# A SwiGLU layer on one core: the last row tile in two column groups, and two of four turned stores behind the next cast

## The chip, the core and the metric

The kernel runs on one core of a Trainium2 chip. The metric is the device time of one execution in microseconds (us). "Before" is the kernel as it stood, "after" the kernel with the change.

## What is computed

```python
B, S, D, F = 1, 2048, 640, 1536      # all bf16, random
def reference(x, w_gate, w_up, w_down):
    g = _silu(x @ w_gate)            # 2048 x 1536
    u = x @ w_up                     # 2048 x 1536
    return (g * u) @ w_down          # 2048 x 640
```

## The kernel before

The 2048 rows are worked through in four blocks of 512 rows (the loop over `sb`, line 271), called stages here. The contraction dimension lies on the 128 partitions: `xT` holds x turned, in 5 slices of 128 of the 640 input columns, and `aT` holds the hidden activations turned, in 12 slices of 128 of the 1536 hidden columns.

**Projections.** For each of the 12 hidden slices, TensorE (PE) makes 5 matmuls for the gate into a PSUM tile `pg` and 5 for the up projection into `pu` (lines 204 and 277 to 278). ScalarE (ACT) applies silu to `pg` (line 221), VectorE (DVE) multiplies by `pu` and writes a slice of `aT` (line 222). The first block has an order of its own in `head()`. The last 4 rows of x are not projected on TensorE: VectorE works them out as dot products with copies of the weights that DMAs have turned (`row_dots`, line 153), spread over the stages with `do_dots(n)`; `row_tail` (lines 167 and 168) writes their activations.

**Output.** The 640 output columns are made in two ways.

- *Columns 512 to 639, turned* (lines 284 to 305). 12 matmuls, with `wd_sb` as the weights, make a tile `po_t` of 128 columns by the block's 512 rows (384 in the last stage). ACT casts it to bf16 (`ot_t`, line 296), DVE turns its 32 x 32 blocks (`ot_q`, line 298), and four DMAs, one for each 32 columns, store it (line 300). These four *turned stores* are issued from ACT's own queue, one after the other: ACT does nothing behind them until they are issued, and the first waits for DVE's turn.
- *Columns 0 to 511* (lines 307 to 334). For each of the block's four row tiles of 128 rows (`j`), 12 matmuls with `aT` as the weights make a PSUM tile `po_a` of 128 x 512 (line 316). ACT casts it (`ot`, line 325), and SyncE (SP) issues its store (line 334). The tag `po_a` has two PSUM buffers, so the third row tile's matmuls need the first row tile's cast to be done, and the fourth need the second's.

The very last row tile is another matter, for there the turned tile holds 384 rows only. Its 640 columns are made in three groups, of 256, 256 and 128 columns (line 312), 12 matmuls each. ACT casts the first two (line 325), DVE the narrow third (`ot_b`, line 328), and SP issues the three stores.

**What sets the order.** Within one engine, instructions run in the order in which they stand. `keep_order` fixes the traced order for DVE and SP at the end of the program (lines 339 and 340), and for PE, ACT and POOL at the end of `head()` alone (lines 266 to 268); behind that, a scheduler places them. SP's queue holds, besides the stores, all large loads; in the first stage a load of x and the turned loads of `w_up` stand behind the fourth row tile's store (lines 335 to 338). DMAs from SP and ACT take eight completion semaphores in turn, and a DMA waits for the previous user of the semaphore that it gets. `_trim` leaves one closing wait on SP (line 414 in the profile), for everything that was started.

Of the kernel before, what the change touches and what calls it, by code (L numbers as in the profile page):

```python
# [10 lines left out]
def _body(  # L11
# [9 lines left out]
    P = nc.NUM_PARTITIONS  # L21
# [5 lines left out]
    B, S0, D = x.shape  # L27
# [10 lines left out]
    DA = 512  # L38
    Q = 32
# [70 lines left out]
    def turn_x(c0, c1, k0=0, k1=KD):  # L110
        s_sl = slice(c0 * P, c1 * P)
        nc.sync.dma_start_transpose(out=xT[:, k0:k1, s_sl], in_=xt_v[s_sl, k0:k1])
# [22 lines left out]
    def turn_w(dst, src):  # L135
        for a in range(0, KF, WT_STEP):
            nc.sync.dma_start_transpose(
                out=dst[:, a : a + WT_STEP, :], in_=src[:, a : a + WT_STEP, :]
            )
# [24 lines left out]
    def row_tail():  # L164
        for _ in dots:
            pass
        nc.scalar.activation(row_s[:], row_g[:], ACT.Silu)
        nc.vector.tensor_tensor(
            out=aT[:, :, S - T : S], in0=row_s[:], in1=row_u[:], op=ALU.mult
        )  # L170
# [3 lines left out]
    def do_dots(n):  # L174
        for _ in range(n):
            next(dots, None)
# [25 lines left out]
    def proj(ps, w_sb, fc, sb, c0, c1, k0=0, k1=KD):  # L202
        for kd in range(k0, k1):
            nc.tensor.matmul(  # L204
                ps[:, c0:c1],
                lhsT=w_sb[:, kd, fc * P : (fc + 1) * P],
                rhs=xT[:, kd, sb * S_BLK + c0 : sb * S_BLK + c1],
                start=(kd == 0),
                stop=(kd == KD - 1),
            )  # L210

    def gu_tiles():
        pg = psum.tile([P, S_BLK], f32, tag="gu", name="pg", bufs=4)
        pu = psum.tile([P, S_BLK], f32, tag="gu", name="pu", bufs=4)
        return pg, pu

    def gate(pg, pu, sb, fc, n_s):

        s0 = sb * S_BLK
        sg = work.tile([P, S_BLK], f32, name="sg")  # L220
        nc.scalar.activation(sg[:, 0:n_s], pg[:, 0:n_s], ACT.Silu)  # L221
        nc.vector.tensor_tensor(  # L222
            out=aT[:, fc, s0 : s0 + n_s], in0=sg[:, 0:n_s], in1=pu[:, 0:n_s], op=ALU.mult
        )
# [46 lines left out]
    for sb in range(NSB):  # L271
        n_s = S_BLK if sb < NSB - 1 else S_BLK - T
        for fc in range(KF):
            if sb == 0 and fc < N_FIRST:
                continue
            pg, pu = gu_tiles()
            proj(pg, wg_sb, fc, sb, 0, n_s)
            proj(pu, wu_sb, fc, sb, 0, n_s)
            gate(pg, pu, sb, fc, n_s)
            if sb > 0 and fc < KF - 2:  # L280
                do_dots(2)


        n_t = (SUB if sb < NSB - 1 else SUB - 1) * P
        po_t = psum.tile([P, n_t], f32, tag="po_b", name="po_t")
        for kf in range(KF):
            nc.tensor.matmul(  # L287
                po_t[:],
                lhsT=wd_sb[:, kf, DA:D],
                rhs=aT[:, kf, sb * S_BLK : sb * S_BLK + n_t],  # L290
                start=(kf == 0),
                stop=(kf == KF - 1),
            )
        ot_t = outp.tile([P, n_t], bf16, name="ot_t")
        ot_q = outp.tile([P, n_t], bf16, name="ot_q")
        nc.scalar.copy(ot_t[:], po_t[:])  # L296
        do_dots(3)
        nc.vector.transpose(out=ot_q[:], in_=ot_t[:])  # L298
        for q in range(P // Q):
            nc.scalar.dma_start(  # L300
                out=out2[
                    sb * S_BLK : sb * S_BLK + n_t, DA + q * Q : DA + (q + 1) * Q
                ].rearrange("(i r) c -> r i c", r=Q),
                in_=ot_q[q * Q : (q + 1) * Q, :].rearrange("r (i c) -> r i c", c=Q),
            )

        for j in range(SUB):
            s0 = sb * S_BLK + j * P
            last = sb == NSB - 1 and j == SUB - 1
            cols = [(0, DA, "po_a")]  # L310
            if last:
                cols = [(0, DA // 2, "po_a"), (DA // 2, DA, "po_a"), (DA, D, "po_b")]
            for c0, c1, tag in cols:
                po = psum.tile([P, c1 - c0], f32, tag=tag, name="po_a")
                for kf in range(KF):
                    nc.tensor.matmul(  # L316
                        po[:],
                        lhsT=aT[:, kf, s0 : s0 + P],
                        rhs=wd_sb[:, kf, c0:c1],
                        start=(kf == 0),  # L320
                        stop=(kf == KF - 1),
                    )
                ot = outp.tile([P, c1 - c0], bf16, name="ot" if c1 < D else "ot_b")
                if c1 < D:
                    nc.scalar.copy(ot[:], po[:])  # L325
                    eng = nc.sync
                else:
                    nc.vector.tensor_copy(out=ot[:], in_=po[:])  # L328
                    eng = nc.sync
                if 0 < j and not last:  # L330
                    do_dots(3)
                if sb == NSB - 1 and j == ROW_J:
                    row_tail()
                eng.dma_start(out=out2[s0 : s0 + P, c0:c1], in_=ot[:])
        if sb == 0:
            turn_x(2 * SUB, 3 * SUB)
            turn_w(wuT, wut_v)
            turn_x(3 * SUB, 4 * SUB)
# [72 lines left out]
def kernel(tc, *args):  # L411
    _body(tc, *args)
    tc.close()
    tc.compile()
    _trim(tc.nc)
# [30 lines left out]
```

## Time and profile before

| what | us |
|---|---|
| time, median of 3 runs (163.05 to 163.59) | 163.4 |
| the profiled execution's own time | 163.25 |
| its span, first to last instruction | 161.9 |
| PE busy | 159.6 |
| DVE busy | 110.5 |
| ACT busy | 42.6 |
| PE, output row tiles (line 316), 216 matmuls | 42.8 |

A row of a timeline has the start, the duration, the engine, the line, the operation and its operands, a count, and in brackets how long the engine was idle ahead of it and what ended that. "SPq" and "ACTq" are the issue of a DMA by that engine, which takes the engine's queue for the duration given; the transfer itself comes later, and "to landing" is the time from the issue to the arrival of its completion. A row of the chain has a start, a duration, an engine, a tile and a line. A row of grouped instructions has its busy time in us, the mean of one in ns, and the idle time ahead. A row of stretches gives a stretch and its length, then the busy time and count of PE, DVE and ACT, the granted clock of TensorE, the busy share of the DMA engines, and GB/s. Matmuls overlap: the next one starts before the one ahead has ended, so a duration of 0.38 goes with a start every 0.216.

### The profile page before, as it was taken

How to read it: one execution, taken by the hardware profiler on the slowest of the kernel's cores; microseconds unless marked ns; L12 is line 12 of the kernel's file. 1: busy time of each engine (PE TensorE's matmuls, PEld its weight loads, DVE VectorE, ACT ScalarE, POOL GpSimd, SP SyncE). 2: the span in 40 equal slices, each digit the busy share in tenths (PEclk: the TensorE clock that was granted, in tenths of full speed). 3: DMA queues.
4: the chain of work that ended last, by engine and by line, in shares of the span. 5: the costliest groups of instructions: out<-in, count | busy, mean ns of one | idle time of the engine just before them, and what ended most of it. 6: DMA issues, size and time to landing. Idle time of an engine off the chain costs nothing.

```text
span 161.9 us, 2159 instructions
## 1 busy us (share of the span) xinstructions
PE 159.6 (99%) x818; PEld 79.9 (49%) x818; DVE 110.5 (68%) x249; ACT 42.6 (26%) x74; POOL 0.6 (0%) x6
## 2 busy tenths in 40 slices
PE   9999999999999999999999999999999999999995
PEld 9885444444444444444444444444444444445454
DVE  1006223599469999989919999979964999993000
ACT  5032222112222222211222322221214222222121
POOL 1000000000000000000000000000000000000000
PEclk9999999999999999999999999999999999999999
DMA  7999999995089992003110000000310000000212
GB/s 228 280 345 348 363 209 241 230 190 100 32 186 139 241 225 58 0 0 34 65 65 4 0 0 2 0 0 4 64 66 32 0 0 0 0 4 0 52 37 73
DMA packets 41209, 15.86 MB, mean 98 GB/s; under 512 B 33264, under 2 KB 41072, under 8 KB 41200
## 3 DMA queue, kind: packets, MB, share of 16 engines
q1 hardware_dynamic: 32832, 14.81, 38.0%
q10 hardware_dynamic: 8368, 0.92, 3.7%
q8 instruction: 6, 0.10, 0.3%
q14 instruction: 3, 0.02, 0.1%
HBM read 6.88 MB, written 2.62 MB: 59 GB/s over the span
## 4 chain that ended last, share of the span: by engine, by line
PE 99%; DVE 0%; issue 0%
PE pu L204 32%; PE pg L204 31%; PE po_a L316 26%; PE po_t L287 6%; PE pg L250 2%; PE pw L182 1%; PE pt L195 1%; DVE ot_b L328 0%; DVE ones L108 0%
## 5 line engine op out<-in xcount | busy, mean ns | idle before, releaser
L204 PE MATMUL pu<-xT,wu_sb 128*128 128x512 bf16 (+2 forms) x260 | 59.3, 362 | 0.0
L204 PE MATMUL pg<-xT,wg_sb 128*128 128x512 bf16 (+2 forms) x240 | 56.9, 370 | 0.0
L222 DVE TENSOR_TENSOR aT<-sg,pu 128x512 bf16<-128x512 f32 (+1 forms) x48 | 32.5, 682 | 32.8 <-PE pu L204 32.8
L221 ACT ACTIVATE sg<-pg 128x512 f32<-128x512 f32 (+1 forms) x48 | 28.4, 597 | 71.1 <-PE pg L204 67.5
L316 PE MATMUL po_a<-wd_sb,aT 128*128 128x512 bf16 (+2 forms) x216 | 42.8, 358 | 0.0
L153 DVE SCALAR_TENSOR_TENSOR prod<-wgT,x_row 128x640 f32<-128x640 bf16 x48 | 39.4, 821 | 1.1
L153 DVE SCALAR_TENSOR_TENSOR prod<-wuT,x_row 128x640 f32<-128x640 bf16 x48 | 39.4, 822 | 1.0
L204 PEld LDWEIGHTS <-wu_sb 128*128 128x128 bf16 x260 | 25.4, 98 | 26.5 <-DMA wu_sb<-in_w_up_dram 0.2
L204 PEld LDWEIGHTS <-wg_sb 128*128 128x128 bf16 x240 | 23.5, 98 | 25.9
L316 PEld LDWEIGHTS <-aT 128*128 128x128 bf16 x216 | 20.7, 98 | 21.6
L325 ACT CAST ot<-po_a 128x512 bf16<-128x512 f32 (+1 forms) x17 | 9.5, 561 | 32.0 <-PE po_a L316 20.9
L287 PE MATMUL po_t<-aT,wd_sb 128*128 128x512 bf16 (+1 forms) x48 | 10.4, 366 | 0.0
L287 PEld LDWEIGHTS <-wd_sb 128*128 128x128 bf16 x48 | 4.7, 98 | 5.1
L328 DVE CAST ot_b<-po_a 128x128 bf16<-128x128 f32 x1 | 0.3, 292 | 9.9 <-PE po_a L316 9.9
L296 ACT CAST ot_t<-po_t 128x512 bf16<-128x512 f32 (+1 forms) x4 | 2.2, 559 | 11.6 <-PE po_t L287 11.6
L153 DVE DVE_READ_ACCUMULATOR prod<-wuT,x_row 128x1 f32 x48 | 4.0, 82 | 0.0
L153 DVE DVE_READ_ACCUMULATOR prod<-wgT,x_row 128x1 f32 x48 | 3.9, 82 | 0.0
L298 DVE STREAM_TRANSPOSE ot_q<-ot_t 128x512 bf16<-128x512 bf16 (+1 forms) x4 | 2.7, 678 | 1.7 <-ACT ot_t L296 1.7
L250 PE MATMUL pg<-xT,wg_sb 128*128 128x256 bf16 (+1 forms) x24 | 3.1, 307 | 0.0
L200 DVE COPY xT<-pt 128x384 bf16<-128x384 bf16 x2 | 0.7, 358 | 3.2 <-PE pt L195 3.2
L250 PEld LDWEIGHTS <-wg_sb 128*128 128x128 bf16 x24 | 2.6, 127 | 0.3
L182 PE MATMUL pw<-ones 128*128 128x128 bf16 x20 | 2.3, 313 | 0.3 <-DVE ones L108 0.3
(15 smaller groups left out, 8.0 us busy)
## 6 DMA issues: line engine op xcount, KB each, us to landing
wd_sb<-in_w_down_dram SPq DMA_DIRECT2D x1, 1920.0 KB, 14.6
out_dram<-ot SPq DMA_DIRECT2D x15, 128.0 KB, 1.7
wg_sb<-in_w_gate_dram SPq DMA_DIRECT2D x2, 640.0 KB, 6.7
wu_sb<-in_w_up_dram SPq DMA_DIRECT2D x2, 640.0 KB, 8.0
x_row<-in_x_dram SPq DMA_DIRECT2D x1, 640.0 KB, 4.9
wg_sb<-in_w_gate_dram SPq DMA_DIRECT2D x3, 128.0 KB, 3.5
wu_sb<-in_w_up_dram SPq DMA_DIRECT2D x1, 384.0 KB, 4.7
out_dram<-ot_q ACTq DMA_DIRECT2D x12, 32.0 KB, 2.1
```

The costliest lines, as they stand in the source:

```text
L153: nc.vector.scalar_tensor_tensor(out=prod[:], in0=wT[:, fc, :], scalar=1.0, in1=x_row[:, t, :], op0=ALU.mult, op1=ALU.mult, accum_out=acc[ ...
L182: nc.tensor.matmul(pw[:, 0:P], lhsT=ones[:].broadcast_to([P, P]), rhs=ones[:].broadcast_to([P, P]), start=True, stop=True,)
L195: nc.tensor.transpose(out=pt[:, kd - k0, :], in_=x_sb[:, c, kd * P : (kd + 1) * P], identity=ident[:],)
L204: nc.tensor.matmul(ps[:, c0:c1], lhsT=w_sb[:, kd, fc * P : (fc + 1) * P], rhs=xT[:, kd, sb * S_BLK + c0 : sb * S_BLK + c1], start=(kd == 0 ...
L221: nc.scalar.activation(sg[:, 0:n_s], pg[:, 0:n_s], ACT.Silu)
L222: nc.vector.tensor_tensor(out=aT[:, fc, s0 : s0 + n_s], in0=sg[:, 0:n_s], in1=pu[:, 0:n_s], op=ALU.mult)
L250: nc.tensor.matmul(pg[:, c0:c1], lhsT=wg_sb[:, kd, wslice(fc, fc + 1)], rhs=xT[:, kd, c0:c1], start=(kd == 0 and c0 == 0), stop=(kd == KD ...
L287: nc.tensor.matmul(po_t[:], lhsT=wd_sb[:, kf, DA:D], rhs=aT[:, kf, sb * S_BLK : sb * S_BLK + n_t], start=(kf == 0), stop=(kf == KF - 1),)
L296: nc.scalar.copy(ot_t[:], po_t[:])
L298: nc.vector.transpose(out=ot_q[:], in_=ot_t[:])
L316: nc.tensor.matmul(po[:], lhsT=aT[:, kf, s0 : s0 + P], rhs=wd_sb[:, kf, c0:c1], start=(kf == 0), stop=(kf == KF - 1),)
L325: nc.scalar.copy(ot[:], po[:])
```

## The change

The last row tile is made in two column groups, of 512 and 128, in place of 256, 256 and 128. And of the four turned stores of a stage two are traced as before, behind the turn, and two behind the cast of the stage's first row tile.

```diff
         nc.vector.transpose(out=ot_q[:], in_=ot_t[:])
-        for q in range(P // Q):
+
+        def store_q(q):
             nc.scalar.dma_start(
...
             )
 
+        late_q = list(range(P // Q // 2, P // Q))
+        for q in range(P // Q // 2):
+            store_q(q)
+
         for j in range(SUB):
             s0 = sb * S_BLK + j * P
             last = sb == NSB - 1 and j == SUB - 1
             cols = [(0, DA, "po_a")]
             if last:
-                cols = [(0, DA // 2, "po_a"), (DA // 2, DA, "po_a"), (DA, D, "po_b")]
+                cols = [(0, DA, "po_a"), (DA, D, "po_b")]
...
                 if c1 < D:
                     nc.scalar.copy(ot[:], po[:])
+                    while late_q:
+                        store_q(late_q.pop(0))
                     eng = nc.sync
```

As built, three stages have on ACT: two turned stores, the first row tile's cast, two turned stores, three casts. The last stage has three turned stores, the first cast, one turned store, three casts.

## The prediction, written before the changed kernel ran

> **What bounds the kernel now.** I read the page first (span, busy times, chain of work that ended last), then the chain in order of time, then the timeline of the last 12 us, since both halves of the change lie there or beside TensorE's work.
>
> ```profile
> span 161.9 us, 2159 instructions
> ...
> PE 159.6 (99%) x818; PEld 79.9 (49%) x818; DVE 110.5 (68%) x249; ACT 42.6 (26%) x74; POOL 0.6 (0%) x6
> ...
> PE 99%; DVE 0%; issue 0%
> ```
>
> ```profile
> 33.15 10.36 PE po_a L316 x48
> ...
> 148.86 11.07 PE po_a L316 x72
> 159.93 0.02 issue
> 159.95 0.29 DVE ot_b L328
> ```
>
> The reader is to see one engine: TensorE is busy 99% of the span, and the chain runs over its matmuls without a gap until 159.93 us. A step counts in two ways only: it makes TensorE work or wait longer, or it moves what stands behind TensorE's last matmul, some 2 us of cast, store and landing. That tail is this:
>
> ```profile
> 156.66 0.59 ACT L325 CAST ot<-po_a 128x512 bf16<-128x512 f32 x1 [2.00 <-PE po_a L316]
> 158.02 0.37 ACT L325 CAST ot<-po_a 128x256 bf16<-128x256 f32 x1 [0.77 <-PE po_a L316]
> 159.33 0.37 ACT L325 CAST ot<-po_a 128x256 bf16<-128x256 f32 x1 [0.94 <-PE po_a L316]
> ```
>
> ```profile
> 159.72 0.33 SPq L334 DMA_DIRECT2D out_dram<-ot  x1
> 159.95 0.29 DVE L328 CAST ot_b<-po_a 128x128 bf16<-128x128 f32 x1 [9.88 <-PE po_a L316]
> 160.27 0.33 SPq L334 DMA_DIRECT2D out_dram<-ot_b  x1
> ```
>
> ```profile
> out_dram<-ot SPq DMA_DIRECT2D x15, 128.0 KB, 1.7
> out_dram<-ot SPq DMA_DIRECT2D x2, 64.0 KB, 1.5
> out_dram<-ot_b SPq DMA_DIRECT2D x1, 32.0 KB, 1.5
> ```
>
> ```profile
> SPq L414 <- DMA out_dram<-ot: 0.5, 1, 0.5
> ...
> SPq L414 <- DMA out_dram<-ot_b: 0.4, 1, 0.4
> ```
>
> The last 64 KB store is issued at 159.72 and lands at about 159.72 + 1.5 = 161.2; the 32 KB store of the narrow tile is issued at 160.27 and lands at about 161.8. The last two rows are SP's own waits: at the close it waits first for the wide store, then 0.4 us more for the narrow one. So the narrow store ends the kernel, and about 0.1 us of closing follows to 161.9.
>
> The profiled execution took 163.25 us, 1.35 more than its span; the median of the three runs is 163.4 (163.05 to 163.59). I work out the difference in the span and add it to the median.
>
> **Part one: one group of 512 columns in place of two of 256.** On TensorE, 24 matmuls of 256 columns go, 12 of 512 come, and 12 weight loads go.
>
> ```profile
> 156.25 0.38 PE L316 MATMUL po_a<-wd_sb,aT 128*128 128x512 bf16 x1
> ```
>
> ```profile
> 159.08 0.83 PE L316 MATMUL po_a<-wd_sb,aT 128*128 128x128 bf16 x12
> ```
>
> ```profile
> 156.46:159.08 2.62, 2.62 (x25) 0.00 (x0) 0.96 (x2) 1.00 0.14 50
> ```
>
> ```profile
> L316 PEld LDWEIGHTS <-aT 128*128 128x128 bf16 x216 | 20.7, 98 | 21.6
> ```
>
> A full stage of 48 matmuls of 512 took 10.36, so one each 0.216 and twelve 2.59. The last of them before the halves started at 156.25, so the halves began at 156.25 + 0.216 = 156.46; the narrow group began at 159.08. They took 2.62 (the row of the stretch: PE busy for all of it, at a granted clock of 1.00). The gain on TensorE is 2.62 - 2.59 = 0.03 us: the columns are the same, and the weight loads of 98 ns were hidden already behind matmuls that start every 2.62 / 24 = 0.109. The narrow group starts at 159.05, its DVE cast at 159.92, and its store could be issued at 160.24 in place of 160.27.
>
> Whether it is depends on SP, which issues the wide store first. The cast of a 512 tile started 156.66 - 156.25 = 0.41 after the start of its last matmul. That last matmul now starts at 156.46 + 11 x 0.216 = 158.84, the cast at 159.25, and it takes 0.59 where the second half took 0.37: it ends at 159.84, where the second half ended at 159.70. From the cast's start to the issue of its store:
>
> ```profile
> 157.27 0.33 SPq L334 DMA_DIRECT2D out_dram<-ot  x1
> ```
>
> 157.27 - 156.66 = 0.61, so the wide store is issued at 159.86 and keeps SP until 160.19 (before: 160.05). Between two issues SP and ACT leave a gap, and a second issue that follows closely can take longer:
>
> ```profile
> 0.00 0.40 SPq L88 DMA_DIRECT2D x_sb<-in_x_dram  x1
> 0.45 1.36 SPq L118 DMA_DIRECT2D wg_sb<-in_w_gate_dram  x3
> ```
>
> ```profile
> 150.01 0.32 ACTq L300 DMA_DIRECT2D out_dram<-ot_q  x1
> ```
>
> ```profile
> 150.38 0.48 ACTq L300 DMA_DIRECT2D out_dram<-ot_q  x1
> ```
>
> The gap is 0.05 (0.40 to 0.45, and 0.33 to 0.38 on ACT). Close issues of 128 KB took (1.36 - 2 x 0.05) / 3 = 0.42 each; ACT's second turned store took 0.48 where the first took 0.32. The trace shows no 128 KB store with a 32 KB one close behind it, so I bound the narrow store's issue. Lower end: SP is free in time and only the 0.03 shows, -0.03. Upper end: it starts at 160.19 + 0.05 = 160.24 and takes 0.48, so it ends at 160.72, where it ended at 160.60: +0.12. I take the row nearest to it, SP's own close issues of 128-row tiles: 160.24 + 0.42 = 160.66, **+0.06**.
>
> Then the landings. The wide store lands at 159.86 + 1.7 = 161.56 (before 161.2), the narrow one at 161.8 + 0.06 = 161.86. The wide one grew 0.34 later but still lands 0.3 ahead, so the narrow one stays last. Below that, the data of the two might share the DMA engines: the wide store's issue is 0.38 ahead of the narrow one's, and in the rows above its landing takes only 0.2 longer, so I add nothing, with 0.2 as the most.
>
> The Trainium skill, page "DMA: Bandwidth & Descriptors", section "Queues, rings and completion order", says that a store's completion count is a strongly ordered write, which lands only after all earlier writes of the same DMA engine. It speaks against the change, for it ties the narrow store's end to a wide store that has twice the bytes and starts 0.14 later. By that rule the narrow store ends at the later of 161.56 and 161.86, so the sum is the same here; if the wide one were late, its whole delay would count, which is the first rival below.
>
> **Part two: two turned stores behind the next cast.** The number of stores and their bytes stay. In the order of the built program three stages have two stores, the cast, two stores; the last stage has three, the cast, one. What ACT did before:
>
> ```profile
> 34.55 1.99 ACTq L300 DMA_DIRECT2D out_dram<-ot_q  x4
> ```
>
> ```profile
> 36.58 0.59 ACT L325 CAST ot<-po_a 128x512 bf16<-128x512 f32 x1 [2.81 <-DVE prod L153]
> 38.36 0.59 ACT L325 CAST ot<-po_a 128x512 bf16<-128x512 f32 x1 [1.20 <-PE po_a L316]
> 40.95 0.59 ACT L325 CAST ot<-po_a 128x512 bf16<-128x512 f32 x1 [2.00 <-PE po_a L316]
> ```
>
> ```profile
> ACT ot L325 <- DMA out_dram<-ot_q: 8.3, 3, 2.9
> ```
>
> Once in each stage, ACT stands idle for the four stores ahead of a cast: 2.81 us in the first stage (put down to DVE, which turns the tile), 8.3 in the other three. That looks like a stall worth removing, but nobody waits for this cast in time: the chain shows TensorE's 48 matmuls from 33.15 in 10.36, the full rate. The cast empties a PSUM buffer of which there are two; the third row tile needs it at 33.15 + 24 x 0.216 = 38.33, and the cast ends at 37.17, 1.16 us early. With two stores ahead, the first tile is ready at about 38.36 - 2.59 = 35.77, the two stores are out at 34.55 + 1.0, so the cast starts at 35.77 and ends at 36.36: 0.8 us sooner, and nothing was late, so 0 gained.
>
> Behind the moved stores: they take ACT from about 35.8 to 36.9 or, at worst, 36.4 to 37.4. Next on ACT is the second cast, which waits for TensorE until 38.36 anyway; then the third and fourth, which wait 2.0. On SP, the first row tile's store goes out 0.8 us sooner and the loads behind the fourth store stay where they are. In the last stage three stores end at 150.01 + 1.4 = 151.4, the first tile is ready at 154.07 - 2.59 = 151.48 by this row, and the fourth store has until then:
>
> ```profile
> 154.07 0.59 ACT L325 CAST ot<-po_a 128x512 bf16<-128x512 f32 x1 [1.49 <-PE po_a L316]
> ```
>
> The moved stores and the tile stores also change places among the eight completion semaphores that DMAs take in turn. A store waits for the semaphore's previous user; in the first stage the fourth turned store now waits for the load of the last rows. That one was issued at 23.0 and took 4.9, so it was done 8 us earlier:
>
> ```profile
> L142 SPq DMA_DIRECT2D x_row<-in_x_dram x1: 582/582/582, 23.0 to 23.0; - x1
> ```
>
> Part two: 0. If this cover were gone (a cast 1.2 us later than now), TensorE would wait for the PSUM buffer, in four places.
>
> **Sum.** -0.03 on TensorE, taken back by SP's queue, and +0.06 at the end: the span becomes 161.9 + 0.06, the profiled execution about 163.31, and from the median 163.4 I forecast **163.46 us**. A difference of 0.3% (0.49 us) is about what a measurement of this kernel can tell from no change.
>
> **Rivals.**
> 1. Slower: the wide store becomes the last to land. For it: its cast is 0.59 and not 0.37, its bytes are twice, and no later work covers it. Against it: 0.3 us of room by the median landing. It decides from a landing of about 2.0 us on; the 128 KB stores reach more than that in this trace, but only in the middle of the kernel:
>
> ```profile
> DMA to landing us min/median/max: 1.5/1.7/3.2
> ```
>
> At 3.2 it lands at 163.06, 1.3 us after the 161.8 of before: 164.7 us. Beyond 0.3% it is from a landing of 2.4 us on, at 162.3. Chance 0.07.
> 2. Slower: a moved store keeps ACT and a cast misses TensorE's need for its PSUM buffer. The second cast must end by 40.92, when the fourth tile starts (33.15 + 36 x 0.216), and ended at 38.95, so the moved stores would have to run 2 us late. Against it: four stores together took 1.99. If each stage lost one 0.5 us store: 163.4 + 4 x 0.5 = 165.4. Chance 0.03.
> 3. Faster: one store fewer shortens the end. The removed store's issue and gap are 0.33 + 0.05; with the 0.03 of TensorE that would be 0.41 less, 163.0. Against it: SP has free time between the issues at 159.72 and 160.27, so the removed issue is not on the path. The Trainium skill, same page, section "Rules for kernel authors", supports this rival: it wants many small transfers joined into a large one and says that under 64 KB one pays mostly overhead. The trace agrees that size costs little (1.5 for 32 and 64 KB, 1.7 for 128 KB), but the store that ends the kernel is the 32 KB one, which is not joined. Chance 0.05.
> 4. The change doesn't do what it says: in the last stage only one store is moved, not two. This changes nothing in the sum, since none of them gains. Chance 0.01.
>
> **How the numbers follow.** The forecast has 0.84: no measurable change. Rival 1 and rival 2 are slower by over 0.3% (0.07 + 0.03). Rival 3 is 0.25% faster, on the bound, so I count 0.02 of its 0.05 as faster, and 0.02 of the forecast, since three runs of before spread by 0.54 us. Faster 0.04, same 0.86, slower 0.10. The forecast's bounds are -0.03 and +0.12 + 0.2, so 163.4 to 163.7, with the runs' spread some 0.25 more each way; down to rival 3's 163.0, and up to 163.95. Rival 1's far end and rival 2 (0.10) are left out.
>
> **What the profile after would show.** TensorE: 12 matmuls of 512 columns in 2.59, the narrow group starting 0.03 sooner, still no gap in the chain. ACT: the first cast of each stage 0.5 to 0.8 us sooner, the second cast still waiting for TensorE. SP: the wide store issued near 159.86, the narrow one ending near 160.66, and at the close a last wait for the narrow store. I am wrong if the last wait is for the wide store, if the narrow store's issue is over 0.5 us, if TensorE shows idle time at the start of a row tile, or if the time moves by more than half a microsecond.

## The result: slower by about 0.2%, which two comparisons put between nothing and 0.3%

| | median, us | runs |
|---|---|---|
| before | 163.39 (163.01 to 163.95) | 22 |
| after | 163.76 (163.37 to 164.44) | 22 |

The ratio after to before is 1.0022, with a 95% interval of 1.0011 to 1.0032: +0.37 us, between 0.18 and 0.52. The forecast was 163.46, no change that can be told, in a range of 163.0 to 163.95. The time lies in the range and within 0.3% of before, but 0.30 above the forecast. A range of 0.95 us holds far more than a change of this size, so the parts of the span test the prediction better than the time does. A second comparison of the two (below) gave 1.0009.

The profiled execution of after took 164.13 us with a span of 162.7 (before 163.25 and 161.9). That is 0.88 longer, more than twice the difference of the medians, so one must ask first where in the span it lies. I cut the span at two places that both kernels have: the first matmul of the up projection, and the start of the narrow tile's cast on DVE. The start of the first, by the timeline of TensorE, before and after:

```profile
3.48 3.13 PE L250 MATMUL pg<-xT,wg_sb 128*128 128x128 bf16 x24
6.57 1.16 PE L204 MATMUL pu<-xT,wu_sb 128*128 128x256 bf16 x9
```

```profile
3.54 3.70 PE L250 MATMUL pg<-xT,wg_sb 128*128 128x128 bf16 x24
7.28 0.39 PE L204 MATMUL pu<-xT,wu_sb 128*128 128x256 bf16 x2
```

The first up projection starts 0.71 us later, at 7.28 instead of 6.57. Most of that is in the 24 matmuls of the first gate tiles, which took 3.13 us in one profile and 3.70 in the other, with the same code and the same loads ahead of them. So 0.71 of the 0.88 lies where the change touches nothing. The chain of after, from 146 us on:

```profile
146.55 1.07 PE pu L204 x5
147.62 1.95 PE po_t L287 x12
149.57 11.04 PE po_a L321 x60
160.61 0.02 issue
160.64 0.29 DVE ot_b L335
```

The output tiles of the last stage took 11.04 where they took 11.07: TensorE's gain of 0.03 is there, and the chain goes from matmul to matmul without an idle stretch, here and in the other stages. From the cast at 160.64 to the end of the span (162.73) it is 2.09 us; before it was 161.85 - 159.95 = 1.90. The last engine rows of after:

```profile
157.38 0.59 ACT L330 CAST ot<-po_a 128x512 bf16<-128x512 f32 x1 [2.00 <-PE po_a L321]
160.01 0.59 ACT L330 CAST ot<-po_a 128x512 bf16<-128x512 f32 x1 [2.05 <-PE po_a L321]
```

```profile
160.62 0.33 SPq L341 DMA_DIRECT2D out_dram<-ot  x1
```

```profile
161.05 0.38 SPq L341 DMA_DIRECT2D out_dram<-ot_b  x1
```

```profile
SPq L421 <- DMA out_dram<-ot: 0.7, 1, 0.7
...
SPq L421 <- DMA out_dram<-ot_b: 0.2, 1, 0.2
```

The narrow cast ends at 160.93, but its store is issued at 161.05, right behind the wide store, and the issue takes 0.38 where it took 0.33. In SP's closing waits the narrow store is still the last to land, now 0.2 us behind the wide one and not 0.4.

### The profile page after: what moved, and what is told of

Read it like the earlier page. It is cut to its first block, busy times and chain, and to the rows that moved or that the text cites. A ratio compares the mean times of both kernels' runs of the same rounds, so it can differ in the third digit from the quotient of the medians.

```text
span 162.7 us, 2131 instructions
## 1 busy us (share of the span) xinstructions
PE 160.3 (98%) x806; PEld 78.8 (48%) x806; DVE 110.5 (68%) x249; ACT 42.4 (26%) x73; POOL 0.6 (0%) x6
## 4 chain that ended last, share of the span: by engine, by line
PE 98%; DVE 0%; issue 0%
PE pu L204 32%; PE pg L204 30%; PE po_a L321 26%; PE po_t L287 6%; PE pg L250 2%; PE pw L182 1%; PE pt L195 1%; DVE ot_b L335 0%; DVE ones L108 0%
## 5 line engine op out<-in xcount | busy, mean ns | idle before, releaser
L321 PE MATMUL po_a<-wd_sb,aT 128*128 128x512 bf16 (+1 forms) x204 | 42.8, 370 | 0.0
L321 PEld LDWEIGHTS <-aT 128*128 128x128 bf16 x204 | 19.5, 98 | 22.8
L330 ACT CAST ot<-po_a 128x512 bf16<-128x512 f32 x16 | 9.4, 586 | 32.3 <-PE po_a L321 24.2
L250 PE MATMUL pg<-xT,wg_sb 128*128 128x256 bf16 (+1 forms) x24 | 3.7, 338 | 0.0
```

The lines of the kernel that those rows point to most:

```text
L250: nc.tensor.matmul(pg[:, c0:c1], lhsT=wg_sb[:, kd, wslice(fc, fc + 1)], rhs=xT[:, kd, c0:c1], start=(kd == 0 and c0 == 0), stop=(kd == KD ...
L321: nc.tensor.matmul(po[:], lhsT=aT[:, kf, s0 : s0 + P], rhs=wd_sb[:, kf, c0:c1], start=(kf == 0), stop=(kf == KF - 1),)
```

## The experiments

All eight ran against the kernel before on the same chip. The table gives the three parts of each profiled span: **head** up to the first up projection, **middle** from there to the start of the narrow cast, **end** from there to the end of the span. (In eight_stores the narrow matmuls stand in another order, so its parts are not quite the same.)

| kernel | head | middle | end |
|---|---|---|---|
| before | 6.57 | 153.39 | 1.90 |
| before, again | 6.86 | 153.38 | 1.88 |
| stores_only | 7.19 | 153.38 | 1.89 |
| after | 7.28 | 153.36 | 2.09 |
| after, again | 6.93 | 153.35 | 2.09 |
| wide_only | 6.50 | 153.36 | 2.07 |
| narrow_on_act | 6.61 | 153.35 | 2.00 |
| two_wide_stores | 7.05 | 153.36 | 2.50 |
| no_wide_store | 7.00 | 153.35 | 1.89 |
| eight_stores | 6.53 | 154.70 | 2.09 |

The middle repeats to 0.02 us and the end to 0.02, while the head varies by 0.8 with the same code. So the profile measures the change to a few hundredths, and the time of a run does so only as a mean over many.

**wide_only**: the change's first part alone.

```diff
-                cols = [(0, DA // 2, "po_a"), (DA // 2, DA, "po_a"), (DA, D, "po_b")]
+                cols = [(0, DA, "po_a"), (DA, D, "po_b")]
```

> The last row tile in 512 and 128 columns, the four turned stores together as before. In the profile after, the end (start of the narrow cast to the end of the span) grew from 1.90 to 2.09 us and TensorE's last row tile shrank by 0.03, so the end costs 0.17; the rest of the longer time stands ahead of 7.3 us, in the first matmuls. Theory Q (the narrow store waits in SP's queue behind the wide store, which is issued 0.4 us before it): this kernel has the whole loss, end 2.05 to 2.13 us, ratio to before about 1.001 (1.000 to 1.003). Rival M (the moved turned stores cost the time): end 2.05 to 2.13 as well, but the ratio is 1.000 to 1.001 and the other part alone carries the rest.

Measured: ratio 0.9996 (0.9973 to 1.0019), end 2.07, middle 153.36. The end has nearly the whole growth, as Q and M both said; the ratio's interval is too wide to tell them apart.

**stores_only**: the second part alone, the last row tile in 256, 256 and 128 as before.

> The turned stores moved as in the change, the last row tile in 256, 256 and 128 columns as before. Theory Q: nothing, end 1.88 to 1.93 us, TensorE without a gap at the row tiles, ratio 0.999 to 1.001. Rival M: ratio about 1.002, with TensorE or a later cast late in some stage. In both, the first cast of each stage starts 0.5 to 0.8 us sooner.

Measured: ratio 0.9992 (0.9968 to 1.0016), middle 153.38, end 1.89. ACT in its first stage:

```profile
35.16 1.04 ACTq L301 DMA_DIRECT2D out_dram<-ot_q  x2
36.39 0.59 ACT L330 CAST ot<-po_a 128x512 bf16<-128x512 f32 x1 [2.00 <-PE po_a L321]
36.40 0.90 ACTq L301 DMA_DIRECT2D out_dram<-ot_q  x2
38.98 0.59 ACT L330 CAST ot<-po_a 128x512 bf16<-128x512 f32 x1 [2.00 <-PE po_a L321]
```

The first cast now waits for TensorE, not for the stores. Against the head (7.19, not 6.57) it stands 0.81 us sooner than the cast at 36.58 of before. The moved stores are issued while the cast runs (both start at 36.4), and the second cast waits for TensorE for 2.00 us. The edit does just what it says, and it is worth nothing: the middle is that of before to 0.01. Rival M falls.

**narrow_on_act**: the changed kernel with the narrow store in ACT's empty queue.

```diff
                     nc.vector.tensor_copy(out=ot[:], in_=po[:])
-                    eng = nc.sync
+                    eng = nc.scalar
```

> The changed kernel, with the narrow store issued from ACT's queue, which is empty at that time, in place of SP's. Theory Q: the narrow store is issued about 0.03 us after its cast, with 0.33 us of issue, and the end falls from 2.09 back to 1.88 to 1.95 us. Rival D (the narrow store's data stand behind the wide store's data on the same 16 DMA engines, whatever queue issues them): its packets begin no sooner than the wide store's end, and the end stays at 2.03 to 2.13 us. Ratio to before 0.999 to 1.001 by Q, about 1.001 by D.

Measured: ratio 0.9992 (0.9967 to 1.0016), end 2.00. The narrow cast and the narrow store, by the timelines of DVE and ACT:

```profile
159.95 0.29 DVE L335 CAST ot_b<-po_a 128x128 bf16<-128x128 f32 x1 [9.85 <-PE po_a L321]
```

```profile
160.28 0.36 ACTq L341 DMA_DIRECT2D out_dram<-ot_b  x1
```

The store is issued 0.03 us behind its cast, as Q said, and the end falls, but by 0.1 and not by 0.2: it lies between the ranges of Q and of D. D as it was put does not hold, for by it the narrow store's packets (the pieces in which the DMA engines move a transfer) begin no sooner than the wide store's end. They began at 161.16, and the wide store's ran until 161.26. In the stretch between, both queues moved data (q10 is ACT's, q1 is SP's; packets, MB, share of the 16 engines):

```profile
q10 hardware_dynamic: 61, 0.02, 66.4%
q1 hardware_dynamic: 14, 0.01, 19.4%
```

What is left of the 0.2 us is taken apart below.

**two_wide_stores**: the same 128 KB as two stores behind the one cast, so the narrow store has two issues ahead of it.

```diff
+                if last and c1 < D:
+                    for h in (0, DA // 2):
+                        eng.dma_start(
+                            out=out2[s0 : s0 + P, h : h + DA // 2],
+                            in_=ot[:, h : h + DA // 2],
+                        )
+                    continue
                 eng.dma_start(out=out2[s0 : s0 + P, c0:c1], in_=ot[:])
```

> The changed kernel, with the wide tile's store cut into two of 256 columns, both issued by SP behind the one cast, so that the narrow store has two issues ahead of it and no more bytes. Theory Q: one more issue of 0.4 us and a gap of 0.05 ahead of the narrow store, the end grows from 2.09 to 2.45 to 2.6 us, ratio to before about 1.004 (1.003 to 1.006). Rival D: the bytes ahead are the same, the end stays within 2.03 to 2.2 us, ratio about 1.001.

Measured: ratio 1.0045 (1.0029 to 1.006), end 2.50, as Q said. SP's timeline, with the narrow cast at 160.41 (0.29 long):

```profile
160.39 0.81 SPq L343 DMA_DIRECT2D out_dram<-ot  x2
161.29 0.38 SPq L348 DMA_DIRECT2D out_dram<-ot_b  x1
```

The narrow tile lies ready from 160.70 and its store waits 0.59 us for SP. One more close issue cost 0.4 us at the end of this kernel, with the same bytes and the same matmuls.

**no_wide_store**: the changed kernel without the store of the last row tile's first 512 columns.

```diff
+                if last and c1 < D:
+                    continue
                 eng.dma_start(out=out2[s0 : s0 + P, c0:c1], in_=ot[:])
```

> The changed kernel without the store of the last row tile's first 512 columns, which stay unwritten; matmuls and casts are as in the changed kernel. If all of the end's growth comes from the wide store ahead of the narrow one (SP's queue and the shared DMA engines together), the end is 1.87 to 1.91 us. If part of it comes from the single 512-column group itself (its longer cast, its bank, the closing waits), the end stays above 1.95.

Measured (one profile, one run of 163.64 us): end 1.89, that of before.

```profile
160.35 0.29 DVE L335 CAST ot_b<-po_a 128x128 bf16<-128x128 f32 x1 [9.85 <-PE po_a L321]
```

```profile
160.66 0.33 SPq L343 DMA_DIRECT2D out_dram<-ot_b  x1
```

The 512-column group and its longer cast cost the end nothing. The 0.2 us comes with the wide store that goes ahead of the narrow one. Leaving that store out also moves the narrow one to another completion semaphore, so this run alone does not say by which way the wide store acts.

**eight_stores**: before, with each turned store cut in two, to see how late a cast may come.

```diff
+            for h0, h1 in ((0, n_t // 2), (n_t // 2, n_t)):
                 nc.scalar.dma_start(
...
```

> The kernel before, with each turned store cut into two halves of the rows: eight issues ahead of the first row tile's cast, the same bytes. Theory of the cover (a cast may come 1.16 us later than before until TensorE waits for its PSUM buffer): if the eight issues take 2.6 to 4.0 us, the cast comes 0.6 to 2.0 us later than before and TensorE waits at the third row tile for what is above 1.16, 0 to 0.9 us in a stage; in the first stage longer, since the last three of the eight take over semaphores from the turned loads of the gate weights. Ratio 1.000 to 1.03. Rival: the casts hold TensorE already, so any delay of the cast shows in full: 0.6 to 2.0 us in each stage.

Measured: ratio 1.0074 (1.0057 to 1.0091), middle 154.70, 1.31 us longer over the four stages. ACT and TensorE in the first stage:

```profile
34.65 3.96 ACTq L301 DMA_DIRECT2D out_dram<-ot_q  x8
38.64 1.07 ACT L326 CAST ot<-po_a 128x512 bf16<-128x512 f32 x2 [4.92 <-DMA out_dram<-ot_q]
```

```profile
32.94 5.34 PE L317 MATMUL po_a<-wd_sb,aT 128*128 128x512 bf16 x23
38.12 0.81 PE L204 MATMUL pg<-xT,wg_sb 128*128 128x512 bf16 x3
39.28 5.34 PE L317 MATMUL po_a<-wd_sb,aT 128*128 128x512 bf16 x24 [0.34 <-ACT ot L326]
```

The cast came 2.06 us later than before, and the third row tile started at 39.28 where it would have started at 38.12: 1.16 late. So 0.9 us of the delay was covered, where the prediction had 1.16: it counted the stage from 33.15, the chain's time, while its first matmul started 0.2 earlier. The rival, by which any delay shows in full, falls. The scheduler put three matmuls of the next block into the wait, so the whole cost is only 0.33 a stage. The wait for the turned loads that was expected in the first stage does not show: its issues take 0.5 each from the second to the last.

This kernel also tells something that it was not made for. In the last stage five of the narrow group's matmuls were put into the wait too, so the narrow tile is ready sooner behind the second half, and the two stores come close:

```profile
161.27 0.33 SPq L335 DMA_DIRECT2D out_dram<-ot  x1
```

```profile
161.70 0.38 SPq L335 DMA_DIRECT2D out_dram<-ot_b  x1
```

From issue to issue it is 0.43 as in after, here behind a store of 64 KB, and the end is 2.09 again. Two close issues cost about as much with half the bytes ahead.

**after_again** and **before_again**: both kernels once more, unchanged.

> The changed kernel once more, beside the unchanged one once more. In the six profiles so far the time to the first up projection (the head, the same code in all six) was 6.5 to 7.3 us, the middle from there to the narrow cast 153.35 to 153.39, and the end 1.89 or 1.90 in the two with 256-column halves against 2.07 and 2.10 in the two with the wide group on one queue. Theory N (the loss is the end alone, and the rest of the 0.37 us between the medians is the head's chance): ratio to before 1.000 to 1.002, about 1.001; end 2.07 to 2.10, middle 153.35 to 153.37, whatever the head. Rival C (something in the change makes the head longer): ratio 1.002 or above again, head above 7.0.

> The kernel before, unchanged, against itself. Theory N: ratio 0.999 to 1.001; head anywhere in 6.4 to 7.4 us, middle 153.37 to 153.40, end 1.88 to 1.91. Rival C: head below 6.7.

Measured: after 1.0009 (0.9995 to 1.0023), before against itself 0.9997 (0.9984 to 1.0009); middles and ends as in the first profiles. Rival C had named a head above 7.0 for after and below 6.7 for before; they were 6.93 and 6.86.

## Why the prediction was right, and which terms were off

The end, behind the narrow cast, taken apart: the wait until the narrow store's issue starts, the issue, from the issue's end to the store's first packet, and from there to the end of the span. The first packet is from the trace's packet records. A store's arrival is counted on one of the eight completion semaphores that DMAs take in turn, in 16 counts; the second column has the number of the semaphore that the narrow store took.

| kernel | semaphore | wait for SP or ACT | issue | to the first packet | first packet to end | sum |
|---|---|---|---|---|---|---|
| before | 105 | 0.03 | 0.33 | 0.50 | 0.74 | 1.61 |
| before, again | 105 | 0.03 | 0.33 | 0.50 | 0.73 | 1.59 |
| stores_only | 105 | 0.03 | 0.33 | 0.50 | 0.74 | 1.60 |
| no_wide_store | 102 | 0.03 | 0.33 | 0.50 | 0.75 | 1.60 |
| two_wide_stores | 105 | 0.59 | 0.38 | 0.50 | 0.73 | 2.20 |
| eight_stores | 105 | 0.18 | 0.38 | 0.50 | 0.73 | 1.80 |
| after | 104 | 0.12 | 0.38 | 0.53 | 0.78 | 1.80 |
| after, again | 104 | 0.12 | 0.38 | 0.52 | 0.77 | 1.79 |
| wide_only | 104 | 0.12 | 0.38 | 0.52 | 0.76 | 1.78 |
| narrow_on_act | 104 | 0.03 | 0.36 | 0.53 | 0.79 | 1.70 |

- *TensorE, -0.03.* Right: 11.04 for 11.07, middle 153.36 and 153.35 for 153.39 and 153.38.
- *The wide store's issue.* Forecast 0.06 ahead of the narrow cast (159.86 and 159.92), measured 0.02 (160.62 and 160.64). The forecast took the cast's start from the third row tile. The fourth cast of a stage starts 0.05 later against TensorE: 2.05 idle where the third has 2.00 in the rows of after. The profile of before had this already, in the fourth cast of its first stage, where the third (at 40.95) has 2.00:

```profile
43.59 0.59 ACT L325 CAST ot<-po_a 128x512 bf16<-128x512 f32 x1 [2.05 <-PE po_a L316]
```

In the trace a separate semaphore instruction on ACT waits for TensorE ahead of each fourth cast; the third has its wait in itself. The fourth tile takes the first tile's bf16 buffer again, so it has one wait more. That this makes the 0.05 is argued; no run takes the wait away. The term was 0.04 to 0.05 too small.
- *The narrow store behind it.* The forecast had 0.38 from issue to issue and then 0.42, together 0.80; measured 0.43 and 0.38, together 0.81. Right in sum, by luck: the gap between the issues was 0.09 and not 0.05, for SP has a wait for the semaphore's previous user between them, and the issue was 0.04 shorter.
- *The landing.* The forecast added nothing, "with 0.2 as the most". From the issue's end to the end of the span after takes 0.05 to 0.06 more than before, in two parts.
  - 0.02 lies ahead of the first packet: 0.52 to 0.53 in the four kernels where the 128 KB store's packets were still running, 0.50 in the six others, two of which have 64 KB stores close ahead. It is there in narrow_on_act too, where the two stores have different queues, so the order within a queue does not make it, and nor does the semaphore, for the 64 KB stores on 104 have 0.50 to 0.51. Why it comes stays open.
  - About 0.03 comes behind it, and most of that goes with the semaphore. With one store fewer the narrow store takes number 104 and not 105, and in every profile the 16 counts of a store on 104 arrive over at least 0.20 us, those of the narrow store on 105 and 102 over 0.17 to 0.18. The two 64 KB halves of one row tile show it with no wide store near: in all five kernels that store such halves, the one on 104 lands 1.22 us behind its issue's end, the one on 102 1.19 to 1.20. No run gave the changed kernel another semaphore.
  - By the Trainium skill, page "DMA: Bandwidth & Descriptors", section "Queues, rings and completion order", a completion count lands only after every earlier write of its DMA engine, across its queues. The order in these traces agrees: in all four kernels the wide store's last count came ahead of the narrow store's first, by 0.10 us in after and 0.01 in narrow_on_act. From the narrow store's last packet to its first count it took 0.18 to 0.20 there and 0.17 to 0.18 in the others, so at most some 0.02 can be laid to that.
- *The wide store does not become the last.* Right: the closing wait for the narrow store still comes last, with 0.2 us.
- *The moved stores, 0.* Right, and by the work named: nobody waited for the first cast. The cover itself was 0.9 us, not 1.16.

The sum of the forecast was +0.06. With the two terms it is 0.06 + 0.05 + 0.06 = +0.17. The profiles give -0.03 in the middle and +0.20 at the end (1.89 in the mean of before's two, 2.09 in that of after's), so +0.17 us, 0.1% of the time. The mechanism was right, and two small terms of the end were too small: the fourth cast's start and the landing.

What stays open is the rest of the first comparison, 0.37 against 0.17. The second gave 0.15 (-0.08 to 0.38), and 0.17 lies just below the first interval. The head's 0.8 us of variation is the only part of the span that moved otherwise, and it did so in before as well. That the change shifts it was not shown, and it can't be ruled out by these heads: seven with some part of the change (6.50 to 7.28) overlap the two of before (6.57 and 6.86). The runs speak against it, for wide_only, stores_only and narrow_on_act, each with a part of the change, were not slower than before (ratios 0.9996, 0.9992 and 0.9992).

Of the rivals, the first (the wide store lands last) and the second (TensorE waits) did not occur. The third (one store fewer shortens the end) came out with the other sign: joining the two halves brought the joined store nearer to the small one that ends the kernel. The fourth, one moved store in the last stage, was no chance but a fact of the program as built, and it changed nothing, as the prediction said. The page "DMA: Bandwidth & Descriptors" of the Trainium skill, section "Rules for kernel authors", wants many small transfers joined; that is not borne out at this place, where two 64 KB stores, each behind a cast of its own, cost 0.2 us less than the joined one. Two 64 KB stores behind one cast (two_wide_stores) cost 0.4 more than it.

No version run here was shown to beat before. Its end, 1.88 to 1.90, is already that of a kernel with no wide store ahead at all, so what these runs show could be added to it is TensorE's 0.03.

## What to carry to other kernels

The stores at the end of a kernel want distance: here a last store issued 0.43 us behind another ended the kernel 0.2 us later, one issued 0.55 behind another cost nothing, and splitting the last tile so that the next-to-last store leaves early was worth more than one store fewer. An idle time in front of an instruction is a gain only if somebody waits for its result: the cast that stood 2.8 us behind four stores had 0.9 us to spare. And where the same code varies by 0.8 us at the start of the span, cut the span at common points and compare the parts.

## What the runs showed of the hardware beyond what was expected

- On SP, an issue that started within 0.1 us behind another took 0.38 us (32 KB) or 0.42 (the second 64 KB store of two_wide_stores) instead of 0.33.
- DMA issues on ACT run beside a cast on ACT: in stores_only both start at 36.4, and the two issues end 0.3 us after the cast.
- Which completion semaphore a store draws shows in its landing: over the ten profiles 0.02 to 0.03 us later on 104 than on 102, in the median of SP's stores of 64 KB (1.22 for 1.19 us behind the issue's end) and of 128 KB (1.37 for 1.35). One store fewer moved the last one from 105 to 104.
- The head of the kernel took 6.50 to 7.28 us in ten profiles of kernels that share this code. Faster matmuls there do not shorten it for sure. In two_wide_stores the 24 gate matmuls took the least of all, 2.60 us (after: 3.70), and then TensorE waited 0.97 for the up weights:

```profile
3.48 2.60 PE L250 MATMUL pg<-xT,wg_sb 128*128 128x128 bf16 x24
7.05 0.39 PE L204 MATMUL pu<-xT,wu_sb 128*128 128x256 bf16 x2 [0.97 <-DMA wu_sb<-in_w_up_dram]
```
